# Pooled attention and MLP on one core: value products as 64x64 and 32-row tiles, V without zero padding

## Chip, cores, metric

One core of one Trainium2 chip. The metric is the device time of one execution in microseconds (us). A profile is one of these executions; its span is about 2 us shorter than the time that is scored.

## The reference, cut to what matters

```python
# q, k, v: [8 batches, 8 heads, 576, 64] float32; pool = 8, Sp = 72
k_p = k.reshape(B, H, Sp, 8, D).mean(axis=3)        # pooled keys   [B, H, 72, 64]
v_p = v.reshape(B, H, Sp, 8, D).mean(axis=3)        # pooled values [B, H, 72, 64]
attn = softmax(q @ k_p.T / 8)                       # [B, H, 576, 72]
x = (attn @ v_p), heads side by side                # [4608, 512]
out = gelu_tanh(x @ w_in[512, 2048]) @ w_out[2048, 512]
```

Each batch has 512 "main" queries; its last 64 are gathered, over all eight batches, into a ninth group, which the text calls the remaining queries (R in the code).

## The kernel before

The 576 pooled rows of a batch (8 heads x 72) lie on partitions in natural order: 64 in one block, then four blocks of 128. A block straddles heads, so V is spread on GpSimd into a zero-padded array `vbd`, in which each pair of heads (128 output rows) has two blocks with zeros where rows of other heads lie. A value product is then 2 full matmuls for each pair of heads, 8 for a batch.

```python
def load_main(b, which, c0, c1, eng):                       # V: one transfer a batch, 128 rows outermost
    t, w0, b0 = (k, 0, 0) if which == "k" else (v, 64, 5)
    src = rows(t, b)[w0 + 128 * c0:w0 + 128 * c1].rearrange("(c p) pl d -> p c pl d", p=128)
    eng.dma_start(out=st[b]["kv"][:, b0 + c0:b0 + c1], in_=src)

def norm(g, j, eng):                                        # cut: sum and reciprocal
    eng.tensor_tensor(out=eb[:, j, 128 * 5 - W:]..., in0=e, in1=r..., op=ALU.mult)

def values(g, half, eng):                                   # cut: the branch of the remaining queries
    for i in range(2):
        pr = 2 * half + i
        for x, (c, n) in enumerate(PARTS[pr]):
            nc.tensor.matmul(out=xo[:, i, :], lhsT=vbd[:, g, n, :], rhs=eT[:, :, c, :],
                             start=(x == 0), stop=(x == 1))

def load_kv(n):                                             # issued by SP in the MLP of the batch two earlier
    load_main(b, "k", 0, 4, nc.sync)
    load_half(b, "k", nc.sync); load_half(b, "v", nc.sync)
    load_main(b, "v", 0, 4, nc.sync)
```

While batch g goes through its MLP on TensorE, the attention of batch g+1 runs beside it: K is pooled on VectorE (DVE), transposed by DMA (`kTd`), copied into `kbd`, and TensorE takes the scores in between two stretches of MLP matmuls. Loads, stores and DMA transposes share the queue that SP fills.

The softmax here doesn't subtract the row's maximum and nothing guards it: scores larger than these inputs give would overflow.

## Time and profile before

| | before |
|---|---|
| time, median of the 3 runs made before the prediction | 301.55 us (301.08 to 301.73) |
| TensorE busy, clock granted | 97%, 0.999 |
| one steady batch, value product to value product | 30.35 us |
| value products of a batch / of the remaining queries | 1.73 / 1.87 us |
| issue of K's load to the first scores that use it (four batches) | 17.2 to 17.4 us |

A matmul group that follows the one before without a gap, as the chain of waits that the prediction quotes shows, means that TensorE sets the time. The last row of the table is read from the start times in the trace: K's load issued at 112.8 us, first scores at 130.1. In before nothing waits for it, because the scores have their turn only then.

### The profile page before, as it was taken

How to read it: one execution, taken by the hardware profiler on the slowest of the kernel's cores; microseconds unless marked ns; L12 is line 12 of the kernel's file. 1: busy time of each engine (PE TensorE's matmuls, PEld its weight loads, DVE VectorE, ACT ScalarE, POOL GpSimd, SP SyncE). 2: the span in 40 equal slices, each digit the busy share in tenths (PEclk: the TensorE clock that was granted, in tenths of full speed). 3: DMA queues.
4: the chain of work that ended last, by engine and by line, in shares of the span. 5: the costliest groups of instructions: out<-in, count | busy, mean ns of one | idle time of the engine just before them, and what ended most of it. 6: DMA issues, size and time to landing. Idle time of an engine off the chain costs nothing.

```text
span 299.3 us, 4581 instructions
## 1 busy us (share of the span) xinstructions
PE 290.7 (97%) x1734; PEld 151.6 (51%) x1734; DVE 146.7 (49%) x241; ACT 158.2 (53%) x242; POOL 55.5 (19%) x71
## 2 busy tenths in 40 slices
PE   7869999999999999999999999999999999999996
PEld 7748844445444544454445444544444544444444
DVE  6895769164706570648073807381639100920012
ACT  1477783667157715672477246724773267426500
POOL 3252033230400240024012400240024000100000
PEclk9999999999999999999999999999999999999999
DMA  7999997995699459947993599049944800351012
GB/s 235 357 387 338 384 350 132 343 279 158 135 279 250 145 127 271 269 146 126 261 297 134 119 249 301 4 107 249 276 147 101 164 36 2 79 114 37 0 70 70
DMA packets 73221, 56.32 MB, mean 188 GB/s; under 512 B 45808, under 2 KB 55408, under 8 KB 73200
## 3 DMA queue, kind: packets, MB, share of 16 engines
q1 hardware_dynamic: 73056, 55.98, 68.2%
q8 instruction: 13, 0.21, 0.3%
q10 hardware_dynamic: 144, 0.07, 0.1%
q14 instruction: 8, 0.07, 0.1%
HBM read 36.70 MB, written 9.44 MB: 154 GB/s over the span
## 4 chain that ended last, share of the span: by engine, by line
PE 91%; DMA 3%; DVE 2%; SPq 1%; POOL 1%; issue 0%; POOLq 0%
PE mm L296 41%; PE mm L301 41%; PE xo L266 4%; DMA q_sb<-in_q_dram 3%; PE sc L208 2%; PE mm L329 1%; POOL eb L231 1%; SPq L98 1%; PE xo L272 1%; PE tp L193 1%; PE sc L213 0%; DVE w_in_b L80 0%; PE tp L240 0%; DVE w_out_b L80 0%; POOL q_b L80 0%; PE xo L255 0%
## 5 line engine op out<-in xcount | busy, mean ns | idle before, releaser
L301 PE MATMUL mm<-w_out_b,gT 128*128 128x512 bf16 x560 | 128.6, 379 | 0.5 <-DVE w_out_b L80 0.5
L296 PE MATMUL mm<-xT,w_in_b 128*128 128x512 bf16 (+1 forms) x640 | 127.6, 358 | 0.5 <-DVE xT L80 0.5
L298 ACT ACTIVATE gT<-mm 128x512 bf16<-128x512 f32 (+1 forms) x160 | 88.4, 555 | 47.0 <-PE mm L296 45.9
L296 PEld LDWEIGHTS <-w_in_b 128*128 128x128 bf16 x640 | 62.2, 98 | 62.6 <-issue 0.5
L301 PEld LDWEIGHTS <-gT 128*128 128x128 bf16 x560 | 53.4, 98 | 59.7 <-DVE w_out_b L80 0.7
L80 DVE COPY osb<-mm 128x512 f32<-128x512 f32 (+2 forms) x37 | 24.3, 658 | 62.9 <-PE mm L301 60.8
L78 ACT CAST xT<-xo 128x1024 bf16<-128x1024 f32 (+1 forms) x18 | 16.6, 966 | 56.8 <-PE xo L266 49.1
L228 DVE TENSOR_REDUCE den<-e 128x8 f32<-128x576 f32 x36 | 26.5, 736 | 38.0 <-ACT e L221 37.9
L148 POOL TENSOR_TENSOR vbd<-kvb,vmask 128x256 bf16<-128x256 bf16 (+2 forms) x40 | 21.2, 553 | 113.5 <-DVE kvb L130 113.4
L128 DVE TENSOR_TENSOR kv<-kv 128x1024 f32<-128x1024 f32 (+3 forms) x20 | 22.4, 1118 | 29.7 <-DMA kv<-in_v_dram 27.7
L231 DVE TENSOR_TENSOR eb<-e,r 128x576 bf16<-128x576 f32 x28 | 27.2, 970 | 1.0
L221 ACT ACTIVATE e<-sc 128x576 f32<-128x576 f32 x36 | 22.5, 650 | 9.6 <-ACT e L221 4.0
L231 POOL TENSOR_TENSOR eb<-e,r 128x576 bf16<-128x576 f32 x8 | 10.1, 1266 | 71.5 <-ACT e L221 41.1
L80 POOL CAST q_b<-q_sb 128x2048 bf16<-128x2048 f32 (+1 forms) x7 | 15.0, 2147 | 4.1 <-DMA q_sb<-in_q_dram 4.1
L208 PEld LDWEIGHTS <-qT 128*128 128x128 bf16 x128 | 10.1, 98 | 7.0 <-ACT qT L78 0.6
L208 PE MATMUL sc<-kbd,qT 128*128 128x144 bf16 x128 | 13.2, 226 | 0.2 <-ACT qT L78 0.2
L266 PE MATMUL xo<-eT,vbd 128*128 128x512 bf16 x56 | 13.2, 379 | 0.0
L129 DVE TENSOR_TENSOR kv<-kv 128x512 f32<-128x512 f32 (+3 forms) x20 | 12.8, 640 | 0.7
L410 PE MATMUL warm<-identb 128*128 128x128 bf16 x112 | 9.1, 249 | 1.4 <-POOL vmask L398 1.4
L494 ACT ACT_TABLE_LOAD x8 | 10.3, 1283 | 0.1
L80 DVE COPY kbd<-kTd 64x288 bf16<-64x288 bf16 x12 | 5.6, 467 | 8.3 <-DMA kTd<-kvb 8.2
L314 ACT ACT_TABLE_LOAD x7 | 9.0, 1283 | 0.1
(55 smaller groups left out, 99.5 us busy)
## 6 DMA issues: line engine op xcount, KB each, us to landing
out_dram<-osb SPq DMA_DIRECT2D x31, 256.0 KB, 6.7
kv<-in_k_dram SPq DMA_DIRECT2D x7, 1024.0 KB, 6.5
q_sb<-in_q_dram SPq DMA_DIRECT2D x7, 1024.0 KB, 5.9
kv<-in_v_dram SPq DMA_DIRECT2D x7, 1024.0 KB, 9.9
w_in_s<-in_moe_w_in_dram SPq DMA_DIRECT2D x4, 1024.0 KB, 13.0
w_out_s<-in_moe_w_out_dram SPq DMA_DIRECT2D x4, 1024.0 KB, 13.8
out_dram<-osb SPq DMA_DIRECT2D x9, 128.0 KB, 2.3
kv<-in_k_dram SPq DMA_DIRECT2D x2, 512.0 KB, 3.9
```

Of the source, the lines that this page charges most:

```text
L78: eng.copy(out=out, in_=in_)
L80: eng.tensor_copy(out=out, in_=in_)
L128: add(out=t[:, :, 0:4, :], in0=t[:, :, 0:4, :], in1=t[:, :, 4:8, :], op=ALU.add)
L148: eng.tensor_tensor(out=vbd[p0:128, b, n0:n1, :].rearrange("p (c r) (hh d) -> p c (r hh) d", c=max(m, 1), d=D), in0=kvb[p0:128, 4 + c0:4 + ...
L208: nc.tensor.matmul(out=o, lhsT=qT[:, j, pr, :], rhs=kbd[:, g, pr].rearrange("d hh s -> d (hh s)"), start=True, stop=True)
L221: nc.scalar.activation(out=e.rearrange("p (x h) s -> p x (h s)", x=2), in_=sc[:, :, 0:4 * Sp], func=ACT.Exp, scale=1.0 / 64.0)
L228: nc.vector.reduce_sum(out=den, in_=e, axis=AX.X)
L231: eng.tensor_tensor(out=eb[:, j, 128 * 5 - W:].rearrange("p (h s) -> p h s", s=Sp), in0=e, in1=r.unsqueeze(2).to_broadcast([128, H, Sp]), ...
L266: nc.tensor.matmul(out=xo[:, i, :], lhsT=vbd[:, g, n, :], rhs=eT[:, :, c, :], start=(x == 0), stop=(x == 1))
L296: nc.tensor.matmul(out=hp[:, 0:c1 - c0], lhsT=w_in_b[:, ko, fo * 128:(fo + 1) * 128], rhs=st[g]["xT"][:, ko, c0:c1], start=(ko == 0), stop ...
L298: nc.scalar.activation(out=gT[:, fo, c0:c1], in_=hp[:, 0:c1 - c0], func=ACT.Gelu_apprx_tanh)
L301: nc.tensor.matmul(out=o, lhsT=gT[:, fo, r * 128:(r + 1) * 128], rhs=w_out_b[:, fo, :], start=(fo == 0), stop=(fo == FO - 1))
```

## The change

Its intent: a head has 72 = 64 + 8 pooled rows. The 64 make a 64x64 tile of the array (64 rows, 64 output columns), so four heads run side by side; the eight left over of two heads share a 32-row tile with all 128 columns. `vbd`, its zeros and five GpSimd products a batch go. In return V must lie by head: rows 0 to 63 of the partitions hold one head, 64 to 127 another.

```diff
     def load_half(b, which, eng):
+        dst = st[b]["kv"][:, 4].rearrange("(m i) pl d -> i m (pl d)", i=2)
         if which == "v":
-            eng.dma_start(out=st[b]["kv"][64:128, 4], in_=rows(v, b)[0:64])
+            for x in range(2):
+                for k2 in range(2):
+                    m = 32 * x + 16 * k2
+                    src = v[b].rearrange("(k2 x k1) (sp pl) d -> k2 x k1 sp (pl d)", k2=2, x=2, pl=8)[k2, x, :, 64:72]
+                    eng.dma_start(out=dst[0, m:m + 16], in_=src)
     def load_main(b, which, c0, c1, eng):
         ...
+            for c in range(c0, c1):
+                src = v[b].rearrange("(k2 x k1) (sp pl) d -> k2 k1 x sp (pl d)", k2=2, x=2, pl=8)[c // 2, c % 2, :, 0:64]
+                eng.dma_start(out=st[b]["kv"][:, 5 + c], in_=src)
     def norm(g, j, eng):
-        eng.tensor_tensor(out=eb[:, j, 128 * 5 - W:]..., in0=e, ...)
+        eng.tensor_tensor(out=eb[:, j, 0:64 * H]..., in0=e[:, :, 0:64], ...)
+        eng.tensor_tensor(out=eb[:, j, 64 * H:]...[:, 0], in0=e[:, :, 64:Sp]..., ...)
+    def values_rem(g, pr, o, blocks, cols):
+        p0 = 64 * (pr % 2) + 32 * (pr // 2)
+        nc.tensor.matmul(out=o, lhsT=vrem[p0:p0 + 32, g]..., rhs=st_eT[0][p0:p0 + 32, blocks, 4, cols], start=True, stop=False)
+    def values_main(g, h, o, blocks, cols):
+        k2, x, k1 = h // 4, h // 2 % 2, h % 2
+        nc.tensor.matmul(out=o[64 * k1:64 * k1 + 64], lhsT=vb[64 * x:64 * x + 64, g, 2 * k2 + k1, :],
+                         rhs=st_eT[0][64 * x:64 * x + 64, blocks, 2 * k2 + k1, cols], start=False, stop=True)
```

Cut: the spread of the eight left-over rows (one small GpSimd product), the order of the head pairs in the scores, four copies in place of two into `kbd`, V's left-over rows on the even and K's last 64 rows on the odd partitions of one shared block (before, each had half of that block), the 1/8 of the pooling moved into the eviction of the value products, and the first batch's left-over rows issued from ACT.

## The prediction

> **What bounds the kernel now.** I read the page first (busy times, slices, chain), then the chain in order of time over one steady batch, the groups by shape, and the DMA view of the start. On the page:
>
> ```profile
> PE 290.7 (97%) x1734; PEld 151.6 (51%) x1734; DVE 146.7 (49%) x241; ACT 158.2 (53%) x242; POOL 55.5 (19%) x71
> PE 91%; DMA 3%; DVE 2%; SPq 1%; POOL 1%; issue 0%; POOLq 0%
> ```
>
> TensorE is busy all the time and is 91% of the chain that ends last; no other engine is above 53%. One steady batch of that chain, in order of time (start, length, what):
>
> ```profile
> 85.46 13.81 PE mm L296 x64
> ...
> 104.16 8.42 PE mm L301 x39
> 112.58 1.73 PE xo L266 x8
> 114.30 1.51 PE mm L301 x7
> 115.81 13.81 PE mm L296 x64
> ```
>
> The reader sees matmuls with no gap, 30.35 us from one L296 to the next. The value products are 8 matmuls of 512 columns, 1.73 us, 216 ns each; six batches have them so. The batch of remaining queries has 64 of 64 columns in 1.87 us (29 ns each), and the first batch two sets of 8 with 256 columns (109 ns each, 0.87 us). All value products are thus 6 x 1.73 + 1.87 + 2 x 0.87 = 14.0 us: the most the change can save is a part of that.
>
> The second resource to look at is the DMA, since the change rewrites the loads of V:
>
> ```profile
> DMA  7999997995699459947993599049944800351012
> q1 hardware_dynamic: 73056, 55.98, 68.2%
> kv<-in_v_dram SPq DMA_DIRECT2D x7, 1024.0 KB, 9.9
> ```
>
> The 16 engines are nearly full in the first 50 us and two thirds busy on average. With them full (17 to 26 us, nearly only packets of 2 KB):
>
> ```profile
> DMA packets 1760, 3.48 MB, mean 387 GB/s; under 512 B 61, under 2 KB 61, under 8 KB 1760
> ```
>
> 387 GB/s over 16 engines is 24.2 GB/s each, so **85 ns for a packet of 2 KB on one engine**. V of a batch is 576 such packets: over 16 engines 36 each, 3.0 us.
>
> **What the Trainium skill says.** (1) "DMA: Bandwidth & Descriptors", section "Why a DMA increments its semaphore by 16 and not by 1": a transfer issued from SP or ACT is split along the slowest dimension (not of size 1) of each side, over the largest number k up to 16 that divides both sizes, on the lowest-numbered k engines; each engine's ring is consumed in order. The trace of before agrees as far as it goes: all its transfers have 64 or 128 rows there, and each of the 146 issues has 16 completion steps (2336 in all). None with k under 16 exists in it. (2) "TensorEngine Tiling (Array Packing)", section "Key Properties": tiles work in parallel, and a change of tiling mode drains the array. The trace agrees. The scores of the remaining queries already use two column tiles:
>
> ```profile
> 220.69 0.65 PE mm L301 x3
> 221.33 0.37 PE sc L213 x8
> 221.71 0.54 PE mm L301 x2
> ```
>
> Matmuls of 144 columns start in pairs 3 ns apart, one pair per 62 ns, so 8 are worth 4 x 62 = 0.25 us; they take 0.37, and the two L301 after them 0.54 where two cost 0.43 elsewhere. So one mode change costs about 0.11 us. (3) "TensorE: Matmul & The Clock Gate", "Part 1": after some 3.4 us of idleness the clock falls to half until the array has been busy again as long. Before has no such pause in its steady part, so it shows nothing of it.
>
> **The change part by part.**
>
> *Value products.* Four matmuls of 32 rows run side by side (one slot of 216 ns), then eight of 64x64 in two fours (432 ns), with three mode changes (3 x 0.11): 0.65 + 0.33 = 0.98 us in place of 1.73. Saved: 0.75 x 6 = 4.5 us. First batch: 3 x 0.109 + 0.33 = 0.66 for 0.87, twice: 0.4 us. Remaining queries: per batch 3 slots of 29 ns and two mode changes, 0.31 us, x 8 = 2.5 us against 1.87: 0.6 us lost. PE alone gains 4.3 us.
>
> *Normalisation.* The multiplication of 128x576 (0.76 to 1.36 us on DVE) becomes 512 elements and a strided op of 64. An op of 64 elements costs about 0.2 us (dup of 64: 182 ns), the first part gets 64 elements shorter (0.07): 0.13 us more, three on DVE in a row, 0.4 us. In before the last transpose of e lands only 0.3 us ahead of the first value matmul (112.41 against 112.71), so some 0.1 to 0.3 us a batch goes to a new wait: 1 to 2 us lost. The five GpSimd products a batch (21.2 us in all) go, but nothing on the path waits for them. Eviction moves from two ACT copies to ACT and DVE side by side; seven L301 matmuls (1.51 us) cover it as now.
>
> *Loads of V.* Here I expect the result. Before, V's main part is one transfer a batch with 128 rows outermost. Now it is four transfers whose source has [2 heads, 64 rows, 2 KB]: the slowest dimension on the DRAM side is **2**. By (1), k is 2, and always the same two engines. The rest of V becomes four transfers of 16 rows with a source [2, 8, 2 KB]: k = 2 again. Per batch each of the two engines gets 4 x 64 + 4 x 8 = 288 packets: 288 x 85 ns = **24.5 us instead of 3.0**. Everything else in the same queue (K, q, stores, transposes) has a share on these two engines and waits behind it.
>
> Engine bound: before, an engine is busy 68.2% of 299.3 = 204 us. Replacing 8 x 3.0 by 8 x 24.5 gives **376 us** of work on each of the two: no schedule can be faster.
>
> Latency: in the steady batch the load is issued at 112.8, and the scores of that batch start at 130.1, 17.3 us later. They need K transposed by DMA, queued behind V. On the slow engine that is K 36 packets (3.1 us), V 24.5, three stores of 8 packets (2.0), the transpose itself (40 packets of 256 B, some 0.7), then 2 us to land and 1 us for the copies into kbd: 33.3 us. So PE waits 16 us for the scores, and, by (3), then runs some 3.4 us at half clock, 1.7 us lost. Per batch **+17.7 us**, for the batches 3 to 7: 5 x 17.7 = 88 us.
>
> Start: the second half of batch 0's queries landed at 14.7 us, queued behind V. V now takes 24.5 where 2 x 1.4 + 0.3 were: +20 us before the first hidden layer, since w_in queues behind too. Batch 1: its V is queued before the transposes of its e; engine time after w_in (ends near 46): K 3, V's rest 2.7, q 2.9, w_out 10.8, V 21.8, together 87, so the value products come near 91 instead of 52, i.e. +39 in all. Batch 2's K transpose follows another 35 us of queue (V 24.5, q, K, stores, q's transpose): scores near 127 instead of 69.6, +58. Sum: 58 + 88 - 3 (net PE gain) = **+143 us**, 301.6 -> about 440. No V is left to load after batch 7, so the last 78 us keep their length.
>
> **The rivals.**
> (a) *All 16 engines are used after all* (the source is reshaped on the way, or successive transfers take other engines). For it: the writer chose these loads, and nothing in before has run with k under 16. Against it: the rule is plain in the skill. Then PE's account stands alone: -4.3 + 1 to 2 (e wait) + 0.3 (more DVE for kbd) = 298 to 300 us, within 2%.
> (b) *Two engines, but the wait is only the engine bound.* Prefetch is three kv buffers deep, so if the queue never drained the time would be 376 us plus the 60 to 78 us at the end that have little DMA work, minus what the end shares: 380 to 400. Against it: each load is issued at the end of the batch before the one that needs it, so latency adds.
> (c) *The four 32-row and the 64x64 tiles don't run side by side*: 12 matmuls of 216 ns and the switches, 2.9 us instead of 0.98, i.e. +1.2 a batch over before. Against it: L213's pairs start 3 ns apart. Hidden beneath (b) or the main line, it would be 7 us more at most.
> (d) *A single engine is faster when the others rest.* The 85 ns come from full engines. At 70 ns V costs 20 us a batch, and the total falls by about 35 us, to 405.
>
> **Range and chances.** I give two-engine loads 0.88. Within it, the engine bound with its tail (380) is the low end, the sum of latencies (440) the middle, and longer queues from stalled issues the high end (475). Rival (a) has nearly all the rest. Over 2% faster would need under 295.5 us, more than PE can give: 0.01.
>
> **What would show each step.** Right: the four V issues a batch land 25 us or more after their issue instead of 9.9; completion steps from the DMA drop from 16 to 2 for those 64 transfers; the DMA row shows long stretches at one or two tenths; idle time of TensorE before the scores of 10 us or more a batch, ended by kbd and behind it by the K transpose; the clock row below 9 in slices after it. The value products between 0.9 and 1.1 us in the chain, the remaining queries' near 2.5. Wrong: V lands within 10 us of issue and the chain stays over 90% TensorE; then the time is near 299. If V is slow but PE waits for V's own pooling and not for K's transpose, the order in the ring was mistaken and the waits are shorter.
>
> Predicted 440 us, range 375 to 475; faster 0.01, same 0.11, slower 0.88.

## The result, and the profile after

**453.97 us** (453.52 to 454.10, 4 runs) against 301.31 us (301.08 to 301.73, 4 runs): ratio 1.5061, 95% interval 1.5035 to 1.5087. A ratio here is always of fast runs in the same rounds, so it isn't quite the ratio of the medians. The output is correct.

The page of after: busy times, the granted clock and the DMA share in 40 slices of the span, and the shares of the chain that ended last.

```profile
PE 305.5 (68%) x1802; PEld 155.5 (34%) x1802; DVE 156.9 (35%) x291; ACT 151.4 (33%) x238; POOL 38.8 (9%) x46
PEclk9657999589569965999579955998599976999999
DMA  5179941961957228361747138441627195504302
SPq 41%; PE 25%; DMA 23%; DVE 8%; issue 3%; ACTq 0%; DVEq 0%
```

TensorE has fallen from 97% to 68% busy and from 91% of the chain to 25%; SP's queue (SPq) and DMA have 64% of it. The DMA row drops to one or two tenths once a batch, and the clock row to five or six tenths after it. The chain in order of time over one steady batch (start, length, what):

```profile
292.41 5.83 DMA kv<-in_k_dram
298.26 4.89 SPq L112
...
303.19 5.15 SPq L112
...
308.38 5.14 SPq L128
...
320.17 6.03 DMA kTd<-kvb
326.23 0.23 DVE kbd L85
...
326.85 0.64 PE sc L209 x4
327.48 0.85 PE mm L331 x2
```

L112 is V's main load. In this batch SP needs about 5 us to issue each of the last two of them, where the first two took 0.5 us each in the trace; then it is held up with the loads of the remaining queries (L128) and three stores, and only at 320.17 can it issue K's transpose. From K's load to the scores it is 34.4 us, where before had 17.3. What the DMA engines did from 298 to 314 us (share in tenths, GB/s, and the sum):

```profile
DMA  1111121111111111111111111111111111111111
GB/s 51 51 51 51 51 92 51 51 51 46 51 51 51 51 51 51 46 46 51 51 51 51 51 41 51 51 51 51 51 51 46 46 51 51 51 51 51 41 51 51
DMA packets 410, 0.82 MB, mean 51 GB/s; under 512 B 18, under 2 KB 18, under 8 KB 409
```

51 GB/s is what two engines move at the 24.2 GB/s each that the prediction worked out (2 x 24.2 = 48.4). 410 packets in 16 us are 26 in a microsecond; a packet of 2 KB has a median of 84 ns here, as on full engines in before. TensorE waits for it (groups: busy us, mean ns | idle before, releaser and its part):

```profile
L331 PE MATMUL mm<-w_out_b,gT 128*128 128x512 bf16 x560 | 140.1, 403 | 0.5 <-DVE w_out_b L85 0.5
...
L209 PE MATMUL sc<-kbd,qT 128*128 128x144 bf16 x128 | 15.9, 259 | 90.3 <-DVE kbd L85 90.1
```

90.1 us of TensorE's idle time before the scores end with `kbd`, the copy of the transposed keys. L331 does the work of before's L301 (mean 379 ns); its 403 ns are the matmuls at the low clock after each wait. What was to be saved is saved: where no wait precedes, the value products (L255: 32-row tiles, L260: 64x64 tiles) take 0.96 us instead of 1.73:

```profile
419.06 0.40 PE xo L255 x4
419.45 0.56 PE xo L260 x8
```

The difference of 152.9 us between the profiled spans divides thus (differences of the times of each group's first value product): start, to the first one, +23.4; from there to batch 1 +14.3; batch 2 +22.0; batches 3 to 6 +20.5, +19.0, +19.8 and +18.7; the remaining queries +15.0; the last batch and the tail +0.2.

### The profile page after: what moved, and what is told of

Same layout as the page of the kernel before. It is cut to its first block, busy times and chain, and to the rows that moved or that the text cites. A ratio compares the mean times of both kernels' runs of the same rounds, so it can differ in the third digit from the quotient of the medians.

```text
span 452.2 us, 4785 instructions
## 1 busy us (share of the span) xinstructions
PE 305.5 (68%) x1802; PEld 155.5 (34%) x1802; DVE 156.9 (35%) x291; ACT 151.4 (33%) x238; POOL 38.8 (9%) x46
## 4 chain that ended last, share of the span: by engine, by line
SPq 41%; PE 25%; DMA 23%; DVE 8%; issue 3%; ACTq 0%; DVEq 0%
SPq L112 18%; PE mm L331 14%; DMA kv<-in_k_dram 9%; DMA kTd<-kvb 8%; SPq L128 8%; SPq L310 6%; PE mm L326 6%; DMA kv<-in_v_dram 6%; SPq L248 4%; SPq L200 4%; DVE den L229 2%; PE sc L209 2%; DVE osb L85 1%; DVE eb L232 1%; SPq L421 1%
## 5 line engine op out<-in xcount | busy, mean ns | idle before, releaser
L331 PE MATMUL mm<-w_out_b,gT 128*128 128x512 bf16 x560 | 140.1, 403 | 0.5 <-DVE w_out_b L85 0.5
L331 PEld LDWEIGHTS <-gT 128*128 128x128 bf16 x560 | 55.8, 103 | 67.4 <-issue 14.1
L209 PE MATMUL sc<-kbd,qT 128*128 128x144 bf16 x128 | 15.9, 259 | 90.3 <-DVE kbd L85 90.1
L268 ACT ACTIVATE xT<-xo 128x1024 bf16<-128x1024 f32 (+1 forms) x12 | 9.5, 812 | 75.0 <-PE xo L260 75.0
L232 POOL TENSOR_TENSOR eb<-e,r 128x512 bf16<-128x512 f32 x8 | 9.1, 1142 | 211.4 <-ACT e L222 150.4
L232 DVE TENSOR_TENSOR eb<-e,r 128x512 bf16<-128x512 f32 x28 | 24.1, 859 | 1.0
L270 DVE TENSOR_SCALAR xT<-xo 128x1024 bf16<-128x1024 f32 (+1 forms) x12 | 11.3, 956 | 18.3 <-PE xo L260 17.9
L85 POOL CAST q_b<-q_sb 128x2048 bf16<-128x2048 f32 (+1 forms) x7 | 12.3, 1764 | 53.5 <-DMA q_sb<-in_q_dram 53.5
L150 PE MATMUL vp<-kv,identf 128*128 128x128 f32 x16 | 3.8, 429 | 17.5 <-DMA kv<-in_v_dram 17.5
L255 PE MATMUL xo<-eT,vrem 32*128 32x64 bf16 (+2 forms) x68 | 5.2, 296 | 15.3 <-DMA eT<-eb 15.1
L158 POOL TENSOR_TENSOR vrem<-kvb,vmask 128x128 bf16<-128x128 bf16 x8 | 3.4, 427 | 103.5 <-DVE kvb L144 103.5
```

The lines of the kernel that those rows point to most:

```text
L85: eng.tensor_copy(out=out, in_=in_)
L209: nc.tensor.matmul(out=o, lhsT=qT[:, j, pr, :], rhs=kbd[:, g, pr], start=True, stop=True)
L232: eng.tensor_tensor(out=eb[:, j, 0:64 * H].rearrange("p (h s) -> p h s", s=64), in0=e[:, :, 0:64], in1=r.unsqueeze(2).to_broadcast([128, H ...
L331: nc.tensor.matmul(out=o, lhsT=gT[:, fo, r * 128:(r + 1) * 128], rhs=w_out_b[:, fo, :], start=(fo == 0), stop=(fo == FO - 1))
```

## The experiments

Twelve kernels ran: the first four (before in the same rounds: median 301.16 us), then four (301.15), three (301.28) and one (301.11). "Wrong" means that V's rows go to other places than the arithmetic expects, with the same bytes and the same instructions otherwise.

### e1: V's main loads cut anew, 64 rows outermost

```diff
-            for c in range(c0, c1):
-                src = v[b].rearrange("(k2 x k1) (sp pl) d -> k2 k1 x sp (pl d)", k2=2, x=2, pl=8)[c // 2, c % 2, :, 0:64]
-                eng.dma_start(out=st[b]["kv"][:, 5 + c], in_=src)
+            for k2 in range(c0 // 2, c1 // 2):
+                for x in range(2):
+                    src = v[b].rearrange("(k2 x k1) (sp pl) d -> k2 x sp k1 (pl d)", k2=2, x=2, pl=8)[k2, x, 0:64]
+                    dst = st[b]["kv"][64 * x:64 * x + 64, 5 + 2 * k2:7 + 2 * k2]
+                    eng.dma_start(out=dst.rearrange("p c pl d -> p c (pl d)"), in_=src)
```

> The changed kernel, with only the loads of V's main part cut another way: still four transfers of 256 KB a batch from the same rows, but each with 64 rows outermost on both sides, so 16 engines by the rule. The remainder of V keeps its four transfers of 16 rows whose source has 2 outermost. Two-engine theory: of the 288 packets a batch on the two engines 256 go to 16 engines, so V costs them 16 x 85 ns + 32 x 85 ns = 4.1 us instead of 24.5; the queue is no longer the bound and the time is 298 to 303 us. Rival (strided rows of two heads, or four issues in place of one, are slow as such, whatever the number of engines): the same bytes, the same strides and the same number of issues stay slow, over 400 us.

Measured: 322.84 us median of 4 (318.82 to 325.60), ratio 1.0622 (1.0594 to 1.0650), correct. Two of the four count as slow, because they are over 1.5% above the fastest; the ratio and the profile are of the fast ones (318.82 and 320.95, mean 319.9). The same bytes in the same number of transfers, and 134 of the 153 us are gone: the shape of these loads is the cause. But 19 us remain that I had not expected. The trace shows where they begin: of the 17.8 us between the profiled spans 8.2 lie ahead of the first value product (25.67 against 17.44 us). K's last block is pooled only when V's left-over rows, which lie in the same block, have landed. Before (L128) and e1 (L144, and TensorE after it):

```profile
7.43 0.42 DVE L128 TENSOR_TENSOR kv<-kv 128x256 f32<-128x256 f32 x1
```

```profile
15.31 0.43 DVE L144 TENSOR_TENSOR kv<-kv 128x256 f32<-128x256 f32 x1 [7.51 <-DMA kv<-in_v_dram]
16.59 0.29 PE L173 MATMUL kT<-identb,kvb 128*128 128x128 bf16 x1 [7.23 <-DVE kvb L157]
```

### e2: only the left-over rows cut anew

```diff
-                    m = 32 * x + 16 * k2
-                    src = v[b].rearrange(...)[k2, x, :, 64:72]
-                    eng.dma_start(out=dst[0, m:m + 16], in_=src)
+                    for k1 in range(2):
+                        m = 32 * x + 16 * k2 + 8 * k1
+                        src = v[b].rearrange(...)[k2, x, k1, 64:72]
+                        eng.dma_start(out=dst[0, m:m + 8], in_=src)
```

> The changed kernel with only the remainder of V cut another way: eight transfers of 8 rows (8 engines) instead of four of 16 rows whose source has 2 outermost. Two-engine theory: 32 of the 288 packets a batch leave the two engines and 4 come back, 28 x 85 ns = 2.4 us less; with eight batches in a row on that path about 19 us less, near 435 us. Rival (the small transfers with their long completion are the cause): most of the loss goes, under 350 us.

Measured: 458.74 us (one run). No gain, but 4.8 us more; the expectation was wrong. With the main loads on two engines, SP stands still behind them, and it spends 0.6 to 0.7 us on each of the four more issues of a batch, some 2.6 us, as much as the 2.4 us that the 8-row form was to save. That this is why nothing was gained is argued, from one run.

### e3: both

> Both re-cuts together: the change to the value products, normalisation and eviction with loads of V that use 16 and 8 engines. Expected by the prediction's account for PE alone: 4.3 us less in TensorE, 1 to 2 us of it lost to the wait for e's last transpose, so 298 to 300 us against 301.3; value products 0.98 us in a steady batch and near 2.5 us for the remaining queries. Rival (the tiles don't run side by side): the value products take 2.9 us a batch and the time is 308 us or more.

Measured: 329.71 us median of 6 (328.15 to 333.12), ratio 1.0974 (1.0938 to 1.1011), correct. Wrong again, and some 10 us worse than e1 (fast runs: mean 329.5 against 319.9). So there is a second cost beside the two engines.

### e4: before with the change's V main loads alone

```diff
-        t, w0, b0 = (k, 0, 0) if which == "k" else (v, 64, 5)
+        if which == "v":
+            for c in range(c0, c1):
+                src = v[b].rearrange("(k2 x k1) (sp pl) d -> k2 k1 x sp (pl d)", k2=2, x=2, pl=8)[c // 2, c % 2, :, 0:64]
+                eng.dma_start(out=st[b]["kv"][:, 5 + c].rearrange("p pl d -> p (pl d)"), in_=src)
+            return
+        t, w0, b0 = (k, 0, 0)
```

> The kernel before with nothing changed but V's main loads, taken from the changed kernel: four transfers a batch with 2 outermost on the DRAM side. The rows land on the wrong partitions, so the output is wrong on purpose; instruction counts and sizes of all engines stay as before. Two-engine theory: 256 packets, 21.8 us a batch on two engines, in place of 32 of V's 36; the same stall as in the changed kernel less the remainder's share: 425 to 445 us. Rival (the slowdown comes from the tiled products, their mode changes or the normalisation): about 302 us.

Measured: 436.15 us (one run, wrong, relative error 1.07), within what was expected. On its page the clock and DMA rows are much like those of after:

```profile
PEclk9658999589579965998589956998599977999999
DMA  5179939453948148552937174632636295605102
```

The arithmetic of before with only these loads is 135 us slower: they make nearly the whole of the 153.

### e7 and e8: 4 and 8 outermost

```diff
-  src = v[b].rearrange("(k2 x k1) (sp pl) d -> k2 k1 x sp (pl d)", k2=2, x=2, pl=8)[c // 2, c % 2, :, 0:64]
+  src = v[b].rearrange("(a g) (sp pl) d -> a g sp (pl d)", g=4, pl=8)[c // 2, :, 32 * (c % 2):32 * (c % 2) + 32]   # e7
+  src = v[b].rearrange("(a g) (sp pl) d -> a g sp (pl d)", g=8, pl=8)[0, :, 16 * c:16 * c + 16]                     # e8
```

> The changed kernel with V's main loads from four heads by 32 rows instead of two by 64: the same number of transfers, packets and bytes, 4 outermost on the DRAM side (wrong rows, so a wrong output on purpose). Two-engine rule: four engines, V's main part costs each 128 x 85 ns = 10.9 us instead of 21.8; seven or eight batches save 10.9 us each, so 365 us, between 355 and 380. Rival (the count of engines is not what matters): 440 to 455 us.

> As the run with four outermost, with eight heads by 16 rows: eight engines, 5.4 us a batch (wrong rows, wrong output on purpose). Two-engine rule: near the run with 64 rows outermost, which measured 322.8 us at 1.4 us a batch: 322 to 335 us. Rival: 440 us or more.

Measured: e7 369.86 us, e8 329.47 us (one run each, wrong, relative errors 0.94 and 1.25). Both lie where they were expected. With 2, 4, 8 and 64 outermost the time is 454, 370, 329 and 320 us (e1: fast runs): it follows the size of the slowest dimension of the source, with the number of transfers, packets and bytes left alone. The completion steps in the traces agree with two, four, eight and sixteen engines: a transfer of V's main part has 3 in after, 5 in e7, 9 in e8 and 16 in e1 (from the totals 2256, 2320, 2448 and 2672; why there is one more than engines stands below). (The step from 8 to e1's 64 isn't clean: e1 has destinations of 64 partitions, see e11.)

### e5: the tiles with heads in natural order

Heads 0 to 3 in rows 0 to 63, 4 to 7 in rows 64 to 127. V then needs two transfers of 512 KB with 64 rows outermost and one for all left-over rows ([8 heads, 8 rows]), three issues a batch instead of eight.

```diff
+            for x in range(2):
+                src = v[b].rearrange("(x c) (sp pl) d -> x sp c (pl d)", x=2, pl=8)[x, 0:64, c0:c1]
+                dst = st[b]["kv"][64 * x:64 * x + 64, 5 + c0:5 + c1]
+                eng.dma_start(out=dst.rearrange("p c pl d -> p c (pl d)"), in_=src)
...
+        x, c, k1 = h // 4, h % 4, h % 2          # and the heads in the order 0 1 4 5 2 3 6 7
```

> The change with other heads in the two halves of the array: heads 0 to 3 in rows 0 to 63 and 4 to 7 in rows 64 to 127, and the eight remaining rows in the order of the heads. V then loads with three transfers a batch (two of 512 KB with 64 rows outermost, one of 64 rows with 8 outermost) in place of the eight of the change and the two of before; the value products, mode changes, normalisation and eviction are those of the change. Theory after the first four runs: two costs were in the loads, the two engines and, once those are gone (322.8 and 329.7 us), the number of issues, 8 and 12 a batch at 0.65 us each on a queue that also waits for earlier landings. With 3 issues both are gone: 297.5 to 301 us against 301.2, value products 0.96 us a steady batch. Rival (what the re-cut loads left, 21 to 29 us, comes from the normalisation's extra op, the bigger eviction or the rows of K and V that alternate): still 315 us or more.

Measured: 306.95 us median of 6 (305.77 to 309.36), ratio 1.0192 (1.0168 to 1.0215), correct; the profiled run is the slowest of them (309.36). 13 us better than e1's fast runs, but 5.8 us above before instead of below it. The steps from batch to batch are 30.5 to 31.3 us, though the value products are shorter.

### e6: before with V in eight transfers of 16 engines

```diff
+            for i in range(4):
+                eng.dma_start(out=st[b]["kv"][64 + 16 * i:80 + 16 * i, 4], in_=rows(v, b)[16 * i:16 * i + 16])
...
+        if which == "v" and c1 - c0 > 1:
+            for c in range(c0, c1):
+                load_main(b, which, c, c + 1, eng)
+            return
```

> The kernel before, right results, with V's loads cut into as many transfers as in the change: four of 128 rows for the main part (one for each chunk) and four of 16 rows for the half chunk, all with a multiple of 16 outermost, so 16 engines each. Issue theory: eight issues in place of two cost what is left in the first re-cut, so 312 to 325 us. Rival (issues are hidden, the queue has room; the rest comes from the tiled products' part of the change): 301 to 304 us.

Measured: 302.00 us median of 4 (301.83 to 302.10), ratio 1.0028 (1.0015 to 1.0041), correct. Eight issues in place of two cost 0.8 us in before. By itself, in before, the number of issues is not the second cost.

### e11: before with V's main load in two halves of 64 rows

A control for what e1, e3 and e5 have in common:

```diff
+        if which == "v":
+            for x in range(2):
+                eng.dma_start(out=st[b]["kv"][64 * x:64 * x + 64, b0 + c0:b0 + c1], in_=src[64 * x:64 * x + 64])
+            return
```

> The kernel before, right results, with each main load of V cut into two transfers of 64 rows (rows 0 to 63, rows 64 to 127), both on the same queue and on 16 engines; nothing else. Half-rate theory: V lands 2.5 us later, which the start pays in full (q's second half is queued behind it) and each steady batch in part (K's copies end 1.9 us before the scores that need them): 303.5 to 308 us. Rival (what the natural-order version lost comes from its compute part): 301 to 302.5 us, as in the run with eight issues.

Measured: 307.02 us median of 6 (305.71 to 309.27), ratio 1.0205 (1.0174 to 1.0236), correct. Nothing but this split, on 16 engines, in the same queue, costs 5.7 us: as much as the whole excess of e5 (which has TensorE's gain in it too, so the costs of e5 add up to more than this split). What the DMA moved while V's main load ran, in before (150.73 to 153.63 us, from the landing of V's small load to that of the main one) and in e11 (155.83 to 160.77):

```profile
DMA packets 1308, 0.92 MB, mean 317 GB/s; under 512 B 977, under 2 KB 977, under 8 KB 1308
```

```profile
DMA packets 1436, 1.01 MB, mean 204 GB/s; under 512 B 1069, under 2 KB 1069, under 8 KB 1436
```

The engines are full in both windows. In e11 the two halves land 2.48 and 2.46 us after each other, 4.94 us for 1 MB; before took 2.90. A packet of 2 KB has a median of 158 to 176 ns in each full microsecond of V in e11, against 84 to 88 ns in before. (Before shows the same for a moment: while its own two 64-row loads run, at 149 us, the median is 147 ns.) K's transpose stands behind V in the queue; from its issue to its landing, in before and in e11:

```profile
DMA to landing us min/median/max: 3.3/3.3/3.3
```

```profile
DMA to landing us min/median/max: 6.1/6.1/6.1
```

In before `kbd` was ready 1.9 us ahead of the scores (158.53 and 160.46 us). In e11 the slack of this batch is used up (165.86 and 166.00), but TensorE doesn't wait here. What it lost lies earlier: the first value product comes 2.1 us later (19.57 against 17.44), and TensorE waits 2.0, 0.65 and 0.17 us before the scores of batches 2, 3 and 4.

The Trainium skill has the reason, in "SBUF — State Buffer", section "Door 1: The DMA port swizzle (why [64,N] ≈ [32,N])": partitions 0 to 63 reach only 8 of the 16 ports by which DMA writes the buffer, 64 to 127 the other 8, and it gives 196 GB/s for 64 partitions against 328 for 128, at 1 MiB. The runs agree in kind and in size: 512 KB in 2.47 us is 212 GB/s for a half, 1 MB in 2.90 us is 361 for the whole. That ports are the mechanism is the page's word; the runs show the rate.

### e9: e5 with the second half of V issued by ACT

```diff
-                eng.dma_start(out=dst.rearrange("p c pl d -> p c (pl d)"), in_=src)
+                q = nc.scalar if x else eng
+                q.dma_start(out=dst.rearrange("p c pl d -> p c (pl d)"), in_=src)
```

> The natural-order version (306.95 us) with one thing changed: of V's two 64-row transfers the one for rows 64 to 127 is issued by ACT, so that on each DMA engine the two lie in two rings. Half-rate theory: in the natural-order trace the packets of V's main part take 150 to 170 ns where a 128-row transfer's take 84, since at any time all engines write into the same half of the partitions; two rings mix the halves again, V lands some 2 us earlier, K's transpose behind it too, the steady batch falls from 30.5-31.3 to 29.6-30.2 us and the start gets back 2 to 3 us: 299 to 303 us. Rival (normalisation and the extra copies into kbd are what is left): 305 to 308 us.

Measured: 304.32 us median of 6 (303.23 to 306.65), ratio 1.0108 (1.0076 to 1.0140), correct. A little above what was expected; the steady steps are 29.5 to 29.9 us, below before's 30.35, for the first time. K's transpose lands in time again:

```profile
DMA to landing us min/median/max: 3.2/3.2/3.2
```

Not because two queues are faster: V's packets still have medians of 160 to 171 ns while they have the engines. The second half has moved away. ACT, which doesn't stand behind SP's transposes, issues it at 138.66 us, and it lands at 143.70, before K's load of that batch is even issued (147.33). Only 512 KB instead of 1 MB stand ahead of K's transpose then. The section "Can I just issue two DMAs to hit both halves?" of the same page says that two such transfers don't add up; in this batch the halves don't run at the same time, so it isn't tested here. What goes with the gain is the earlier time.

What keeps it above before is the start: the first value product comes at 21.20 us instead of 17.44 (the diff leaves out that in the first batch ACT issues its half after its table load). From there to the end it takes 278.2 us, and before 279.6.

### e10: e9 with two smaller repairs

All small normalisation products on GpSimd, and the remaining queries' value products in three stretches (a zero product opens each sum, then all 32-row tiles, then all 64x64 tiles) so that the mode changes twice instead of sixteen times.

> The two-ring version with two more edits meant to beat both kernels: the 64-element op of the normalisation always on GpSimd, which has room, and the value products of the remaining queries in three stretches (a zero product that opens the sums, all 32-row tiles, all 64x64 tiles) in place of sixteen mode changes. Expected against the two-ring version: 13 mode changes of 0.11 us less, 1.4 us, and 0.3 us of e's wait in each of six batches: 2 to 3 us less, 297 to 300 us. Rival (the wait for e isn't on the path, or GpSimd's 0.69 us op ends later than DVE's 0.3 us one): within 1 us of the two-ring version.

Measured: 304.89 us median of 6 (303.17 to 307.07), ratio 1.0119 (1.0086 to 1.0152), correct. Wrong: nothing gained over e9. The second repair does what it should:

```profile
239.79 0.33 PE xo L300 x4
240.12 0.24 PE xo L255 x32
240.36 0.64 PE xo L260 x64
```

1.2 us, where e9 takes 2.6 us for the same (eight pairs of 0.14 and 0.19 us). The first one takes it back: an op of 64 elements has 0.69 us on GpSimd in after, and TensorE now waits 4.0 us in four places for the transposed e (in e9 1.3 us in two).

### e12: a try at the start

e9, the three stretches of e10 with the small op back on its engine, and in the first batch both halves of the queries queued ahead of V, V's second half issued after the copies of K, and V pooled after the first two normalisations.

> A try at a version that beats both kernels: the kernel of e9 (natural head order, two rings for V) with two changes. (1) The remaining queries' value products in three stretches as in e10, but with the 64-element normalisation op back on the engine of the 512-element one. (2) In the first batch both halves of the queries are queued ahead of V, V's second half is issued by ACT only after the copies of K, and V is pooled after the first two normalisations. If the start of e9 (first value product at 21.2 us, 3.8 us later than in before) was late because V's loads at half rate competed with the queries, the first value product comes at 17.5 to 19 us and the time at 299.5 to 302.5 us. If the extra normalisation op and the order of DVE's work were the cause, it stays at 20.5 to 22 us and the time at 303 to 305. The remaining queries' products: about 1.3 us instead of 2.6.

Measured: 306.04 us median of 5 (305.31 to 306.52), ratio 1.0162 (1.0146 to 1.0177), correct. The first value product came at 25.52 us, later than either theory had it. The chain (start, length, what):

```profile
17.15 0.45 PE tp L244 x5
17.60 3.28 issue
20.88 3.75 PE vp L150 x16
24.63 0.96 PE sc L209 x8
25.59 0.33 PE xo L255 x4
```

The first half of the theory holds: the queries are cast from 9.86 us on instead of 12.72 in e9, and the transposes of the two e that the first value product needs start at 15.39 and 17.15 us instead of 18.40 and 20.17. From the cast to the first of them it takes 5.5 us, in e9 5.7, so the order of DVE's work did little: the queries were late because of V. But V now shares full DMA engines with `w_in`, and TensorE, which pools part of V (vp), stands still for 3.3 us (the chain calls it issue; in the trace it is a semaphore wait of 3.5 us ahead of vp) and then works at a granted clock of 0.50 (mean of 21 to 26 us). From the first value product to the end it takes 276.5 us, 3.1 less than before. With before's start that would be 298 us; this is an estimate from the two numbers (17.44 + 276.5, and 4.1 us for what lies outside, as in before: 301.1 - 297.0), and no version reached it. None of the twelve beats before.

## Why the prediction was right

**The bound now and what could be won.** Right in kind. TensorE set the time, and the value products went from 1.73 to 0.96 us (predicted 0.98), the remaining queries' from 1.87 to 2.6 (2.5). So rival (c), tiles not side by side, is out. One reading was wrong: not six but seven batches have eight products of 512 columns (L266 has 56 matmuls in before), so all value products take 15.7 us, not 14.0, and TensorE's own gain comes to about 5 us, not 4.3. (The last transpose of e is 0.3 us ahead, as said, but at 112.11 against 112.41.) Not all of this gain came out: from the first value product to the end e9, with the change's work on TensorE as it is, takes 1.4 us less than before, and e12, with fewer mode changes, 3.1.

**Two engines.** Right, and shown from several sides: 51 GB/s in after, e4 (loads alone: +135 us), e1 (loads undone: -134 us), e7 and e8 (4 and 8 outermost). The sign that I named was misread: completion steps of a V transfer are 3, not 2 (2256 in all, 129 x 16 + 64 x 3). The section that I cited says why (that the rings are consumed in order stands in another section of that page, "Queues, rings and completion order"): the issuing sequencer writes what is missing to 16 at once, and this is the third step. Rival (a) is out. So is (d): the packets have a median of 84 ns on the two engines with the others at rest, no less than on full ones.

**24.5 us on each engine, latency instead of capacity.** Right in the sum, different inside, and so in part by luck. Predicted from K's load to the scores: 33.3 us; measured 34.4 to 34.9 in five batches. In the batch shown, 5.6 us to the end of K's bytes, 21.3 us with two engines at work (298.0 to 319.3), 0.9 to the issue of the transpose, 6.0 to its landing, 0.6 to the scores. I had let the transpose queue early behind V; in fact SP itself is stopped, because it can't issue V's last transfers, and so the transpose is issued only when V is through. At the start, too, the path was another: the chain of after runs through V itself, which lands at 33.5 us and is pooled by TensorE from 33.6, and not through the queries behind it. Rival (b), 380 to 400 us, falls with it: the engines' capacity wasn't the limit.

**The waits' size.** The term that was too small is the steady batch: +17.7 us predicted; the four groups after batch 2 have +18.7 to +20.5. From one value product to the next batch's scores it is 17.0 to 17.6 us longer (TensorE's idle time there is 17.7 to 18.2 us; I had 16), and from the scores to the value product 1.4 to 3.0 us longer (I had 1.7 for the low clock). "Batches 3 to 7: 88 us" became 94.0 (20.5 + 19.0 + 19.8 + 18.7 + 15.0 + 1.1), with TensorE's gain already in it, while I had taken 3 off again. Start and batch 2 were +58 predicted, at batch 2's scores; measured it is +57.1 there (126.62 against 69.57) and +59.8 at its value product, by way of +23.4 (20 predicted) and, at batch 1, +37.8 (39). Sums: 143 predicted (301.6 + 143 is 445, which I wrote as about 440), 153 measured.

**The clock.** Right in kind: the first four scores after the wait take 0.64 us instead of 0.25, the first two L331 0.85 instead of 0.43, and the clock row drops after each stretch of waiting. In the batch shown TensorE is idle from 309.2 us on, and the granted clock is 0.50 from 312.6 to 329.7, 2.9 us into the work. In batches 3 to 5 it stays at 0.50 for 5.9, 2.8 and 4.9 us after the scores have begun; half of these times is 2.9, 1.4 and 2.4 us, which accounts for nearly all of the 1.4 to 3.0 above, where I had 1.7 for every batch.

**The small normalisation op.** Its size was right as a rule: the median on DVE is 0.22 us (the mean 0.31, because one takes 1.9). It isn't free in after: the chain holds one of 1.83 us in the first batch and two of 0.2 us in most later ones.

**What it didn't see.** Rival (a) was worked out as "all 16 engines, then 298 to 300 us". e1 and e3 show that this was too simple: with V's main loads on all 16 engines 19 us and more were left. e11 shows one part by itself: destinations of 64 partitions run at 0.59 of the rate (212 against 361 GB/s), and this alone costs 5.7 us. Another part is the wait for V's left-over rows, which lie in the block that K's pooling also reads: 8.2 us of e1's excess arise before its first value product, where DVE waits 7.5 us for them. The last of them is issued at 4.0 us and lands at 15.2. In e3, with 8 engines for these rows but twice the transfers, ACT issues the last one only at 10.8 us, and TensorE waits 6.5 us at the same place; in e5, with one transfer for all of them, it doesn't wait there. So the number of engines isn't all of it; what makes them late in e1 was not tested. In one steady batch of e1 K's pooling starts 10.7 us after K's load, where before needs 7.7. The rest of e1's and e3's excess I have not taken apart.

## What to carry to other kernels

Before you change how an operand lies in the buffer, write down for each load the slowest dimension on both sides and the partitions it reaches: the first gives the number of DMA engines, the second the rate, and here they weighed 134 and 6 us against a gain of 3 on TensorE. Here a load that lay ahead of a small latency-bound transfer in the same queue was paid in that transfer's wait, not in bandwidth; issuing half of it at an earlier, quiet moment helped here (e9 against e5). And this kernel, with its engine 97% busy, had only 2 us of slack beside it, so look for the slack before you count the gain.

## What the Trainium skill lacked or had wrong

- "DMA: Bandwidth & Descriptors" gives no figure for how long transfers on few engines hold their issuer. In the batch of after shown above SP issues V's first six transfers in about 0.6 us each and then needs 4.9 and 5.1 us for the last two, and everything behind them in its program waits; SP's queue has 41% of the chain.
- The same page's rule to use all 16 engines names one condition, the outermost dimension. Other rows of that table ask for 128 partitions and for one transfer in place of two on disjoint halves, but none says what the half costs; that stands in "SBUF — State Buffer", where I didn't look: 64 rows outermost gave 16 engines and still 4.94 us for 1 MB instead of 2.90, a packet of 2 KB taking 158 to 176 ns instead of 84 to 88. A pointer from the rule itself to that section is missing.
- The same page's table of rules says that spreading DMAs over SP and ACT doesn't help and only saves issue time. It speaks of bandwidth, and for that no run here differs. It doesn't mention what the issue time can be worth where the issuer stands still: e9 is at 1.0108 of before where e5 is at 1.0192, with ACT issuing its half 10 us ahead of SP's (138.66 and 149.01 us in one batch).
- "TensorEngine Tiling (Array Packing)" says that a change of mode drains the array, but gives no cost. Here 12 value products in three slots of 216 ns took 0.96 us, so the three changes cost 0.31 us together, some 0.10 each; sixteen changes in the remaining queries made 2.6 us out of what took 1.2 with three stretches.
